# Folding a block-diagonal feature map into two projection weights: pairs of 64-row TensorE tiles with 64 columns in place of four 32-row tiles with 32 columns

## Chip, cores and metric

One core of a Trainium2 chip. The metric is the device time of one execution in microseconds (us). All runs whose times are compared by a ratio are in the fast state, and the granted TensorE clock was 0.998 to 1.0 in them; one execution of the kernel before, at a clock of 0.562 and 354.4 us, is left out. Experiments 9 to 11 are single runs, whose state is unknown: 10 and 11 had a clock of 1.0, and 9 had 0.984, for a reason told there. Single runs of the same kernel lie up to 1.7 us apart.

## The reference, cut to what matters

```python
q, k, v = (qkv[0], qkv[1], qkv[2])            # x @ wqkv, S = 2048, D = 512, 32 heads of 16
pq = jnp.einsum('bhsd,hdf->bhsf', q, w_phi)   # one 16 x 16 feature map per head
pk = jnp.einsum('bhsd,hdf->bhsf', k, w_phi)
phi_q = concatenate([softmax(pq), softmax(-pq)])   # phi_k likewise
...                                            # linear attention, then a gMLP branch and a gate
```

As `(x @ wq) @ w_phi = x @ (wq @ w_phi)`, the kernel folds `w_phi` into the two weights once, and never computes q or k. The "fold" is this small product, done for wk and for wq: 512 x 512 times a block-diagonal matrix with blocks of 16 x 16.

## The kernel before

```python
NT = 16; NDT = 4; P = 128; CH = 512            # 16 row tiles of 128, 4 slices of D
halves = [slice(64 * h, 64 * h + 64) for h in range(2)]
# wqkT: transposed wq and wk; wphi: w_phi as 4 block-diagonal tiles of 128 x 128, zeros elsewhere
...
def fold(qk):
    dst = (wq_p if qk == 0 else wk_p)[:].rearrange("p dt n -> p (dt n)").rearrange(
        "p (m r f) -> p r m f", r=4, f=32)
    pair = zp_tile()                            # two PSUM banks, from the ring of the z tiles
    banks = [pair[:, 0, :], pair[:, 1, :], pq_tile([P, CH])[:, :], pq_tile([P, CH])[:, :]]
    for m in range(NDT * NDT):
        dt, kc = divmod(m, NDT)
        for r in range(4):                      # four row tiles, one bank each
            rows = slice(32 * r, 32 * r + 32)
            nc.tensor.matmul(
                banks[r][:, m * 32:(m + 1) * 32],
                lhsT=wqkT[rows, qk * 4 + kc, dt * P:(dt + 1) * P],
                rhs=wphi[rows, kc, rows], start=True, stop=True)
    ...                                         # ScalarE copies the pair now, the other two banks later
```

The fold for wk lies among the z2 matmuls (L191) at about 26 us, the one for wq at about 36. Later in the kernel, ScalarE stores the output in bursts of four tiles and then goes on with the exponentials of the q projection:

```python
def ba_store(acc, tt, c0=0, c1=D, on_dve=False, on_sp=False):
    ...
        nc.scalar.activation(out=ob[:, :], in_=acc, func=AF.Copy, scale=g_inv[:, tt:tt + 1])   # L531
        (nc.sync if on_sp else nc.scalar).dma_start(out=dst, in_=ob[:, :])                     # L532
...
def ba_step(tt):
    ...
    if tt == group[-1]:                         # groups of four row tiles
        for t in group:
            ba_rem(accs[t][:, :], t)
        attn_tile_64(tt + 2)
        for t in group:
            ba_store(accs[t][:, :], t)          # four stores from ScalarE's own queue
...
for i in range(NT - 1):
    if i + nq < NT:
        q_tile(i + nq, bank_tile(q_bank))       # L355 matmuls, L359 exponentials; one bank for all q tiles
    gg_next(...)                                # L454
    ...
```

## Time and profile before

| view | figure |
|---|---|
| time | 206.62 us, median of 3 runs (206.25 to 206.85) |
| span of the profiled execution | 204.5 us |
| TensorE busy | 98% of the span, 95% of the chain that ended last |
| both folds on that chain | 2 x 0.59 us |
| instructions, all engines | 3978 |
| transfers of instructions on DMA queue q8 | 12, of 16,384 bytes each |

How to read it: TensorE is the bound from end to end, so a change counts by what it does to the moments at which TensorE's matmuls start. The lines themselves are in the prediction. The last row of the table played no part in the prediction, and should have.

### The profile page before, as it was taken

The numbers are of one execution on the slowest core, as the hardware profiler recorded it, in microseconds if no ns is written. First come the engines' busy times: TensorE is split into PE (matmuls) and PEld (weight loads), VectorE is DVE, ScalarE is ACT, GpSimd is POOL, SyncE is SP. The second block draws the span as 40 slices with busy tenths as digits, with TensorE's granted clock in tenths as the row PEclk, the third lists the DMA queues.
The fourth block names the chain that finished last, engine by engine and source line by source line (L and its number), as shares of the span: only waits on it lengthen the run. The fifth ranks groups of instructions, "written<-read, shape, count | busy, mean of one in ns | idle before, by whom it ended". The sixth has DMA issues, their size and how long they took to land.

```text
span 204.5 us, 3978 instructions
## 1 busy us (share of the span) xinstructions
PE 199.6 (98%) x1539; PEld 119.7 (59%) x1557; DVE 130.4 (64%) x283; ACT 74.6 (36%) x122; POOL 45.7 (22%) x76
## 2 busy tenths in 40 slices
PE   7999999999999999999999999999999999999994
PEld 3666666655665555656565666555555555665642
DVE  4467484837977587979797789555566645633332
ACT  3466678796222333332424042222351136002303
POOL 3020202021523325334242442222204220200000
PEclk9999999999999999999999999999999999999999
DMA  6997599999998027940422229763568458652833
GB/s 184 269 209 133 118 237 212 239 216 217 235 276 185 3 38 179 290 93 16 75 48 45 51 38 119 139 124 70 100 161 80 90 113 183 63 96 51 156 64 104
DMA packets 89932, 27.22 MB, mean 133 GB/s; under 512 B 84185, under 2 KB 89913, under 8 KB 89913
## 3 DMA queue, kind: packets, MB, share of 16 engines
q1 hardware_dynamic: 87600, 24.81, 63.1%
q10 hardware_dynamic: 2312, 2.16, 3.7%
q8 instruction: 12, 0.20, 0.4%
q14 instruction: 8, 0.06, 0.1%
HBM read 4.15 MB, written 2.10 MB: 31 GB/s over the span
## 4 chain that ended last, share of the span: by engine, by line
PE 95%; DMA 2%; issue 1%; SPq 0%; DVE 0%
PE mm L454 37%; PE zp L191 18%; PE mm L355 13%; PE mm L515 8%; PE mm L395 7%; PE mm L509 7%; DMA w_z<-in_B_w_in_dram 2%; PE kvacc L411 2%; PE at L467 2%; PE mm L520 1%; PE zp L307 0%; PE at L478 0%; SPq L117 0%; SPq L119 0%; PE pq L307 0%
## 5 line engine op out<-in xcount | busy, mean ns | idle before, releaser
L454 PE MATMUL mm<-z2all,wspT 128*128 128x344 bf16 x512 | 79.9, 309 | 0.0
L454 PEld LDWEIGHTS <-wspT 128*128 128x128 bf16 x512 | 49.0, 98 | 25.3
L191 PE MATMUL zp<-w_z,xT 128*128 128x344 bf16 (+1 forms) x254 | 38.1, 310 | 0.3 <-DMA w_z<-in_B_w_in_dram 0.3
L359 ACT ACTIVATE eq<-mm 128x512 bf16<-128x512 f32 x32 | 17.4, 594 | 51.4 <-PE mm L355 25.7
L363 DVE TENSOR_REDUCE zs<-eq 128x64 f32<-128x1024 bf16 x16 | 19.5, 1220 | 20.0 <-ACT eq L359 20.0
L191 PEld LDWEIGHTS <-xT 128*128 128x128 bf16 x254 | 24.4, 98 | 12.1 <-issue 0.3
L359 ACT ACTIVATE ek<-mm 128x512 bf16<-128x512 f32 x32 | 17.3, 601 | 27.1 <-PE mm L355 27.1
L459 DVE SCALAR_TENSOR_TENSOR ucat<-mm,bT,z1all 128x344 bf16<-128x344 f32 x32 | 17.4, 544 | 15.1 <-PE mm L454 15.1
L372 POOL TENSOR_TENSOR eq<-eq,ratio 128x512 bf16<-128x512 bf16 x16 | 16.9, 1055 | 44.6 <-DVE ratio L371 36.6
L531 ACT ACTIVATE ob<-mm,g_inv 128x512 bf16<-128x512 f32 (+1 forms) x15 | 10.1, 679 | 33.1 <-PE mm L520 28.5
L363 DVE TENSOR_REDUCE zs<-ek 128x64 f32<-128x1024 bf16 x16 | 19.2, 1208 | 2.8 <-ACT ek L359 2.8
L515 PE MATMUL mm<-wspT,uT 128*128 128x512 bf16 (+2 forms) x85 | 20.1, 367 | 0.0
L355 PEld LDWEIGHTS <-xT 128*128 128x128 bf16 x128 | 12.2, 98 | 12.0
L372 POOL TENSOR_TENSOR ek<-ek,ratio 128x512 bf16<-128x512 bf16 x16 | 16.9, 1055 | 2.2 <-DVE ratio L371 1.7
L395 PE MATMUL mm<-wv_sb,xT 128*128 128x512 bf16 x64 | 16.4, 380 | 0.0
L355 PE MATMUL mm<-wq_p,xT 128*128 128x512 bf16 x56 | 16.0, 380 | 0.4
L355 PE MATMUL mm<-wk_p,xT 128*128 128x512 bf16 x61 | 16.1, 379 | 0.2
L509 PE MATMUL mm<-wspT,oT 128*128 128x512 bf16 (+2 forms) x61 | 15.6, 365 | 0.4
L209 DVE BATCH_NORM_STATS2 bn<-z2all 128x6 f32<-128x344 bf16 x32 | 14.9, 502 | 0.0
L206 ACT ACTIVATE z2all<-zp 128x688 bf16<-128x688 f32 x16 | 11.8, 743 | 7.6 <-PE zp L191 7.6
L260 ACT ACTIVATE z1all<-zp 128x688 bf16<-128x688 f32 x16 | 11.9, 743 | 5.1 <-PE zp L191 4.7
L515 PEld LDWEIGHTS <-uT 128*128 128x128 bf16 x85 | 8.1, 98 | 9.4 <-issue 0.2
(77 smaller groups left out, 142.0 us busy)
## 6 DMA issues: line engine op xcount, KB each, us to landing
out_dram<-ob ACTq DMA_DIRECT2D x12, 128.0 KB, 2.4
wspT<-in_B_w_out_dram SPq DMA_DIRECT2D x2, 640.0 KB, 4.9
w_z<-in_B_w_in_dram SPq DMA_DIRECT2D x2, 344.0 KB, 5.0
wv_sb<-in_A_wqkv_dram SPq DMA_DIRECT2D x2, 256.0 KB, 4.4
wspT<-in_A_wo_dram SPq DMA_DIRECT2D x2, 256.0 KB, 3.9
out_dram<-ob SPq DMA_DIRECT2D x3, 128.0 KB, 1.8
w_z<-in_B_w_in_dram ACTq DMA_DIRECT2D x2, 172.0 KB, 3.7
w_z<-in_B_w_in_dram SPq DMA_DIRECT2D x2, 172.0 KB, 3.8
```

The costliest lines, as they stand in the source:

```text
L191: nc.tensor.matmul(zp[:, j, 0:n], lhsT=xT[:, dt, tt * P:(tt + 1) * P], rhs=wt[:, dt, j * HF:j * HF + n], start=(dt == 0), stop=(dt == NDT ...
L209: nc.vector.bn_stats(out=bn6[:, tt, j, :], in_=z2v[:, j, :])
L260: nc.scalar.activation(out=z1all[:, tt, :].rearrange("p (j n) -> p j n", j=2), in_=zp[:, :, 0:HF], func=AF.Gelu_apprx_tanh,)
L355: nc.tensor.matmul(ps[:, :], lhsT=xT[:, dt, tt * P:(tt + 1) * P], rhs=w[:, dt, :], start=(dt == 0), stop=(dt == NDT - 1))
L359: nc.scalar.activation(out=e[:, :, a, :], in_=ps[:, :].rearrange("p (h f) -> p h f", f=DH), func=AF.Exp, scale=1.0 - 2.0 * a)
L363: nc.vector.tensor_reduce(out=z[:].rearrange("p h a -> p (h a)"), in_=e[:].rearrange("p h a f -> p (h a) f"), axis=AX.X, op=ALU.add,)
L372: nc.gpsimd.tensor_tensor(out=e[:, :, 1, :], in0=e[:, :, 1, :], in1=ratio[:, :, None].to_broadcast([P, H, DH]), op=ALU.mult)
L395: nc.tensor.matmul(v_ps[:, :], lhsT=xT[:, dt, tt * P:(tt + 1) * P], rhs=wv_sb[:, dt, :], start=(dt == 0), stop=(dt == NDT - 1))
L454: nc.tensor.matmul(gp[:, 0:HF], lhsT=wspT[:, st, tt * P:(tt + 1) * P], rhs=z2all[:, st, j * HF:(j + 1) * HF], start=(st == 0), stop=(st == ...
L459: nc.vector.scalar_tensor_tensor(out=ucat[tt % NU][:, c0 + j * HF:c0 + (j + 1) * HF], in0=gp[:, 0:HF], scalar=bT[:, tt:tt + 1], in1=z1all[ ...
L509: nc.tensor.matmul(acc, lhsT=oTs[tt][:, g, :], rhs=wo_t[:, g, c0:c1], start=start and g == 0, stop=stop and g == NG - 1)
L515: nc.tensor.matmul(acc, lhsT=uTs[tt][:, i + ft, :], rhs=w_main[i][:, ft, c0:c1], start=start and ft == 0, stop=False)
```

## The change

A row tile is a matmul on 32 or 64 of the 128 rows that the other matmuls use; a round is one matmul on each of the tiles that run side by side; a weight load is the LDWEIGHTS instruction for the `lhsT` operand, of which the trace has one per matmul (1493 of each in the changed kernel).

The intent: half as many matmuls and weight loads for the same result. A 64-row tile takes four heads at a time, two such tiles run side by side (3 to 4 ns apart in the trace after), and each streams 64 columns; of the four 32 x 32 blocks of `wphi` that it multiplies, the two off the diagonal are zeros.

```diff
@@ -297,24 +297,24 @@
 
     def fold(qk):
         dst = (wq_p if qk == 0 else wk_p)[:].rearrange("p dt n -> p (dt n)").rearrange(
-            "p (m r f) -> p r m f", r=4, f=32)
+            "p (m a f) -> p a m f", a=2, f=64)
         pair = zp_tile()
-        banks = [pair[:, 0, :], pair[:, 1, :], pq_tile([P, CH])[:, :], pq_tile([P, CH])[:, :]]
+        odd = [pq_tile([P, CH])[:, :] for _ in range(2)]
         for m in range(NDT * NDT):
             dt, kc = divmod(m, NDT)
-            for r in range(4):
-                rows = slice(32 * r, 32 * r + 32)
+            cols = slice(m % 8 * 64, m % 8 * 64 + 64)
+            for a, rows in enumerate(halves):
                 nc.tensor.matmul(
-                    banks[r][:, m * 32:(m + 1) * 32],
+                    (odd[m // 8] if a else pair[:, m // 8, :])[:, cols],
                     lhsT=wqkT[rows, qk * 4 + kc, dt * P:(dt + 1) * P],
                     rhs=wphi[rows, kc, rows], start=True, stop=True,
                 )
 
-        def take(out, in_):
-            nc.scalar.copy(out=out, in_=in_.rearrange("p (m f) -> p m f", f=32))
-
-        nc.scalar.copy(out=dst[:, 0:2], in_=pair[:, :, :].rearrange("p r (m f) -> p r m f", f=32))
-        return [lambda: take(dst[:, 3], banks[3]), lambda: take(dst[:, 2], banks[2])]
+        def take(h):
+            nc.scalar.copy(out=dst[:, 1, 8 * h:8 * h + 8], in_=odd[h].rearrange("p (m f) -> p m f", f=64))
+
+        nc.scalar.copy(out=dst[:, 0], in_=pair[:, :, :].rearrange("p r (m f) -> p (r m) f", f=64))
+        return [lambda: take(1), lambda: take(0)]
 
     with tc.manual_schedule(engines={mybir.EngineType.PE, mybir.EngineType.Activation}):
         z2_first_two()
```

Passages that no trace of this case bears out are cut from the recorded prediction, and the cuts are marked: the reading of the two paces (25 and 33 ns), the bounds drawn from it, figures from outside this case, and the cost of a stalled z tile. No term of the sum is cut: it came to -20 to +22 ns per fold, 206.62 plus or minus 0.04, put at 206.6 us. Where columns are divided by 2.4, the trace of the kernel before shows that pace: neighbouring matmuls of 344 columns start 145.8 ns apart, those of 512 columns 215.8, so 0.417 ns per column and 2.5 ns besides. The 8.3 ns of the first rival is a quarter of the 33 ns round; that it is a cost of issue was my assumption and not shown. That weight loads hide rests on the 16 of L478: 93 ns each as recorded, they lie within 0.47 us, and their matmuls hold the chain for 0.19. "Drain" is what a gap between two starts holds beyond the first matmul's own columns.

> **What bounds the kernel now.** I read the page first (busy time, slices, the chain that ended last), then the chain in order of time around the two folds, then the timeline of the fold's own matmuls, and at last ScalarE's part in it.
>
> ```profile
> span 204.5 us, 3978 instructions
> ...
> PE 199.6 (98%) x1539; PEld 119.7 (59%) x1557; DVE 130.4 (64%) x283; ACT 74.6 (36%) x122; POOL 45.7 (22%) x76
> ...
> PEclk9999999999999999999999999999999999999999
> ...
> PE 95%; DMA 2%; issue 1%; SPq 0%; DVE 0%
> ```
>
> TensorE is busy 98% of the span at full granted clock in every slice, and 95% of the chain that ended last is TensorE. So only time taken off TensorE's own stream can shorten the run; anything on another engine counts only if TensorE begins to wait for it. The fold's share of that stream is the next question. The chain in order of time, around the second fold (start us, length us, what):
>
> ```profile
> 26.74 9.45 PE zp L191 x64
> 36.19 0.12 PE zp L307 x2
> 36.31 0.01 PE pq L307 x2
> ...
> 36.76 0.02 PE pq L307 x2
> 36.78 7.12 PE zp L191 x48
> ```
>
> L307 is the fold. It runs twice (for wk at 26.15, for wq at 36.19), and each time it holds the chain for 36.78 - 36.19 = 0.59 us. Both together are 1.18 us, 0.6% of the span. This is the whole stake: a fold that cost nothing at all would save 0.6%, which is under the 2% that makes a verdict of faster. The question left is whether the new form is some tenths of a microsecond shorter or longer.
>
> How the present fold is paced shows in the timeline of the first one (start us, us from first start to last end, engine, line, what, how many):
>
> ```profile
> 26.25 0.18 PE L307 MATMUL zp<-wphi,wqkT 32*128 32x32 bf16 x2
> 26.26 0.17 PE L307 MATMUL pq<-wphi,wqkT 32*128 32x32 bf16 x2
> 26.27 0.17 PE L307 MATMUL zp<-wphi,wqkT 32*128 32x32 bf16 x2
> ...
> 26.50 0.19 PE L307 MATMUL zp<-wphi,wqkT 32*128 32x32 bf16 x2
> 26.52 0.19 PE L307 MATMUL pq<-wphi,wqkT 32*128 32x32 bf16 x2
> 26.53 0.19 PE L307 MATMUL zp<-wphi,wqkT 32*128 32x32 bf16 x2
> ```
>
> Two rows (zp and pq) are one round of the four 32-row tiles. Up to about 26.30 a round takes 25 ns (zp rows start at 26.25 and 26.27; the raw starts are 3 to 4 ns apart within a round, then a pause of 15). From 26.30 on a round takes 33 ns (26.50, 26.53; raw starts 8 to 9 ns apart, with no pause). [...] Nine rounds are in the first regime, seven in the second; from the first start (26.085) to the last (26.559) it is 0.474 us.
>
> What a pair of 64-row tiles does, this kernel shows elsewhere, in the attention product on two halves. Its chain:
>
> ```profile
> 145.53 0.54 PE mm L520 x4
> 146.07 0.19 PE at L478 x16
> 146.26 0.97 PE mm L355 x4
> ```
>
> L478 is 16 matmuls of 64 rows and 34 columns, alternately on the two halves: 0.19 / 8 = 24 to 25 ns per pair of halves, with a raw distance of 3 ns inside a pair. L520 is four matmuls of 64 rows and 512 columns in 0.54 us, where four one after the other take 0.86 us. So the two halves run at once, and the weight loads hide.
>
> [...] 16 matmuls of 344 columns take 2.33 us, 145.8 ns each, against 143.3 + 2.5[...]. [...] here loads of 32, 64 and 128 rows by 128 columns last 91, 93 and 98 ns as recorded, so a 64-row load is no dearer than a 32-row one. [...] the last z2 matmul before the first fold starts at 25.843 and the first fold matmul 0.242 us later, of which 0.143 is its own 344 columns, so some 98 ns are drain; after the fold there are 112 ns from the last start to the next, 13 of them its own 32 columns, so again 98.
>
> **The change part by part.**
>
> Removed: 64 matmuls and 64 weight loads per fold, of 32 rows and 32 columns. Added: 32 of each, of 64 rows and 64 columns. The lower or upper 64 rows of wphi are block diagonal with zeros outside, so the result is the same. The rounds are 16 before and 16 after; what changes is that a round is two matmuls of 64 columns and not four of 32.
>
> Cost of a new round. [...] Streaming is 64 / 2.4 = 26.7 ns per tile[...], plus the 2.5 ns that the 344-column matmuls show: 29.2 ns. A second estimate from the nearest width in the trace: 68 columns on 128 rows, eight in 0.26 us, 32 ns each, 28.3 of them streaming; taken as it stands, that is an upper figure for a round. So 15 steps take 438 to 480 ns, plus 3 for the second tile of the last round: 441 to 483 ns, against 474.
>
> Drain on the way in: unchanged, 98 ns (the same change from 128 rows to a smaller row tile). Drain on the way out: 98 plus the last 64 columns, 26.7 ns, instead of 13.3: 13 ns more.
>
> Sum per fold, from the last start before to the first start after: before 242 + 474 + 112 = 828 ns; after 242 + (441 to 483) + 125 = 808 to 850 ns. So -20 to +22 ns per fold, and -0.04 to +0.04 us for both. The number of instructions saved is real (128 of TensorE's 3,096)[...].
>
> ScalarE's copies: one of 1024 elements and two of 512 per fold, before and after.
>
> ```profile
> L314 ACT CAST wk_p<-pq x2: 580/580/581, 31.0 to 33.4; 128x512 bf16<-128x512 f32 x2
> ...
> L316 ACT CAST wk_p<-zp x1: 1007/1007/1007, 26.8 to 26.8; 128x1024 bf16<-128x1024 f32 x1
> ```
>
> (1007 - 580) / 512 = 0.834 ns per element. [...] I expect 1007 and 580 again. They lie beside TensorE's work in any case.
>
> Moved: the banks hold other parts of the result, but the same copy (the pair of banks) is still first, and the two single banks are still taken later, the second of them first, beside the same z1 tiles. The first use of wk is at 43.7, ten microseconds after its last copy; of wq at 70.0. Nothing waits for either.
>
> So the sum is 206.62 plus or minus 0.04, and I put it at 206.6.
>
> **The rivals.**
>
> First, the fold is issue-bound as a whole, and half the instructions halve it: 32 x 8.3 = 0.27 us in place of 0.47, -0.2 us each, -0.4 in all, some 206.2. For it: the 8.3 ns regime is there. Against it: the 34-column pairs of L478 need 25 ns per pair though issue would allow 16.5[...].
>
> Second, the two halves don't overlap with these operands, or weight loads show: 32 x 29 to 32 = 0.93 to 1.02 us, about +0.5 us each, +1.0 in all, 207.6. Against it: L478 and L520, with halves 3 ns apart.
>
> Third, ScalarE or a bank gets late and TensorE waits. ScalarE is busy 16 of the 20 us from 26 to 46, and the page shows no wait of TensorE for it there. As nothing about its copies changes in size or order, I give this little weight[...].
>
> Fourth, the compiler's order on VectorE and GpSimd shifts a little with the shorter fold. TensorE's wait for both is almost nil now, so this could cost or give some 0.2 us at most, an estimate from the small TensorE idle times (0.4 us the largest group).
>
> **Range and chances.** The mechanism gives a shift far below what runs differ by: before, three runs lie between 206.25 and 206.85. The range therefore is that scatter, widened a little for the first, third and fourth rivals: 206.0 to 207.1. A verdict of faster needs -4.1 us, over three times the whole cost of both folds; slower needs +4.1, four times the second rival. Faster 1%, same 98%, slower 1%.
>
> **What would show it.** In the timeline of the changed kernel, rounds of two 64-row matmuls start 29 to 32 ns apart, evenly, with no second regime, and with 3 to 4 ns inside a round. In the chain each fold holds 0.57 to 0.61 us. ScalarE's copies are 1007 and 580 ns. The gap after the last fold matmul is about 125 ns. A round of 17 ns would prove the first rival, 58 or more the second; a wait of TensorE for ScalarE between 26 and 46 us the third; another order of work on VectorE the fourth. The prediction is wrong if the time leaves 206.0 to 207.1 in undisturbed runs.

## The result, and the profile after

The changed kernel took 206.65 us (median of 6 runs, 206.58 to 207.67), the kernel before 206.45 us (median of 6, 205.94 to 206.85). A ratio here and below is the mean time of one kernel's fast runs over that of the other's of the same rounds, so it is not quite the ratio of the medians: 1.002, 95% interval 0.9996 to 1.0044. By the measure of 2% this is the same, and inside the predicted range. Still the medians moved up by 0.2 us and the means by 0.4, where the working had said 0.04 at most. An unchanged time lies within the interval, so the times alone don't call for a cause. Part of the means' rise is one run, 207.67 us with a span of only 205.0: 1 us more than in the other five lies outside its recorded span, and without it the means differ by 0.24. But the trace did show something.

The page of the changed kernel (its head, busy times, the instruction queue, and the chain by engine):

```profile
span 204.9 us, 3869 instructions
...
PE 200.7 (98%) x1493; PEld 119.9 (58%) x1493; DVE 130.4 (64%) x283; ACT 74.6 (36%) x122; POOL 45.7 (22%) x76
...
q8 instruction: 11, 0.18, 0.4%
...
PE 93%; DMA 2%; ACT 2%; ACTq 1%; SPq 0%; issue 0%; DVE 0%
```

TensorE is still busy 98%. The chain of before had no ScalarE in it; now 2% is ScalarE and 1% its queue. And there is one transfer of instructions fewer. First the folds themselves, in the chain in order of time:

```profile
26.75 9.45 PE zp L191 x64
36.20 0.13 PE zp L307
...
36.77 7.11 PE zp L191 x48
```

and in the timeline of the first fold:

```profile
26.32 0.19 PE L307 MATMUL zp<-wphi,wqkT 64*128 64x64 bf16 x1
26.32 0.19 PE L307 MATMUL pq<-wphi,wqkT 64*128 64x64 bf16 x1
26.35 0.19 PE L307 MATMUL zp<-wphi,wqkT 64*128 64x64 bf16 x1
26.35 0.19 PE L307 MATMUL pq<-wphi,wqkT 64*128 64x64 bf16 x1
```

A round of two matmuls takes 29 ns, evenly through the fold (raw starts 26.318, 26.347, 26.376; 3 to 4 ns within a round). The fold holds the chain for 36.77 - 36.20 = 0.57 us instead of 0.59. From the last z2 matmul's start before a fold to the next one's start after it:

| | into the fold | first to last start | out of the fold | sum |
|---|---|---|---|---|
| before, two folds | 242, 242 ns | 474, 475 | 112, 112 | 828, 829 |
| after, two folds | 243, 242 ns | 450, 451 | 122, 123 | 815, 816 |

So each fold became 13 ns shorter. (The step after that, between the first two z2 matmuls behind a fold, takes 156 to 157 ns instead of the usual 146, in both kernels alike.) ScalarE's copies are what they were, as the lines' own instructions show:

```profile
L314 ACT CAST wk_p<-pq x2: 580/580/580, 31.0 to 33.4; 128x512 bf16<-128x512 f32 x2
...
L316 ACT CAST wk_p<-zp x1: 1007/1007/1007, 26.8 to 26.8; 128x1024 bf16<-128x1024 f32 x1
```

Then where is the rise? I laid TensorE's start times of the two traces side by side, matmul by matmul. The changed kernel starts its steady stream 20 ns late (its first weights landed later), gains 13 + 13 ns at the folds and is 7 ns ahead from 37 us on. At 152 us it falls 0.383 us behind in a single step, and it ends 0.365 us behind. The chain of the changed kernel at that step (start, length, what):

```profile
149.21 0.70 ACT ob L531
...
149.93 0.78 ACTq L532
...
150.84 1.09 ACT eq L359 x2
...
151.98 1.02 PE mm L355 x4
```

and the timelines of ScalarE and of TensorE in the kernel before at the same place:

```profile
149.22 0.69 ACT L531 ACTIVATE ob<-mm,g_inv 128x512 bf16<-128x512 f32 x1 [0.42 <-ACT ob L531]
149.94 0.34 ACTq L532 DMA_DIRECT2D out_dram<-ob  x1
150.40 1.08 ACT L359 ACTIVATE eq<-mm 128x512 bf16<-128x512 f32 x2 [0.49 <-ACT ob L531]
...
151.60 1.03 PE L355 MATMUL mm<-wq_p,xT 128*128 128x512 bf16 x4
```

Up to 149.9 us both are alike to 10 ns. Then the issue of the fourth output store holds ScalarE's queue for 0.78 us instead of 0.34. The two exponentials behind it start at 150.84 instead of 150.40 and end at 151.93 instead of 151.48. They free the one bank of the q projection; before, that was 0.12 us early enough for the next q matmuls (151.60), and now those wait.

Nothing of this touches the fold, 110 us earlier. What differs at that moment is on the DMA queues, between 149 and 151 us. Before:

```profile
q10 hardware_dynamic: 329, 0.30, 46.9%
q1 hardware_dynamic: 550, 0.13, 31.8%
...
out_dram<-ob ACTq DMA_DIRECT2D x2, 128.0 KB, 1.9
```

After:

```profile
q1 hardware_dynamic: 533, 0.13, 82.4%
q10 hardware_dynamic: 135, 0.12, 52.4%
q8 instruction: 1, 0.02, 3.0%
...
out_dram<-ob ACTq DMA_DIRECT2D x2, 128.0 KB, 2.8
```

A transfer of 16,384 bytes of instructions lies among the stores (it starts at 149.36 us and takes 0.97), and the stores land 0.9 us later. The packets of q1, SyncE's transposes at that time, are slower too: as many bytes take 82.4% of the engines' time instead of 31.8%. In the trace of before such transfers lie at 140.16 and 157.10 us, and none meets this burst. (One meets a later burst, at 190.9 us, without cost to TensorE: see after the experiments.)

### The profile page after: what moved, and what is told of

It reads as the page before. It is cut to its first block, busy times and chain, and to the rows that moved or that the text cites. A ratio compares the mean times of both kernels' runs of the same rounds, so it can differ in the third digit from the quotient of the medians.

```text
span 204.9 us, 3869 instructions
## 1 busy us (share of the span) xinstructions
PE 200.7 (98%) x1493; PEld 119.9 (58%) x1493; DVE 130.4 (64%) x283; ACT 74.6 (36%) x122; POOL 45.7 (22%) x76
## 4 chain that ended last, share of the span: by engine, by line
PE 93%; DMA 2%; ACT 2%; ACTq 1%; SPq 0%; issue 0%; DVE 0%
PE mm L454 35%; PE zp L191 18%; PE mm L355 13%; PE mm L515 8%; PE mm L395 7%; PE mm L509 6%; DMA w_z<-in_B_w_in_dram 2%; PE kvacc L411 2%; PE at L467 2%; ACT ob L531 1%; PE mm L520 1%; ACTq L532 1%; ACT eq L359 1%; PE zp L307 1%; SPq L117 0%
## 5 line engine op out<-in xcount | busy, mean ns | idle before, releaser
L515 PE MATMUL mm<-wspT,uT 128*128 128x512 bf16 (+2 forms) x85 | 20.1, 367 | 0.0
L509 PE MATMUL mm<-wspT,oT 128*128 128x512 bf16 (+2 forms) x68 | 16.6, 366 | 0.0
L515 PEld LDWEIGHTS <-uT 128*128 128x128 bf16 x85 | 8.1, 98 | 9.4 <-issue 0.2
```

The lines of the kernel that those rows point to most:

```text
L509: nc.tensor.matmul(acc, lhsT=oTs[tt][:, g, :], rhs=wo_t[:, g, c0:c1], start=start and g == 0, stop=stop and g == NG - 1)
L515: nc.tensor.matmul(acc, lhsT=uTs[tt][:, i + ft, :], rhs=w_main[i][:, ft, c0:c1], start=start and ft == 0, stop=False)
```

## The experiments

Theory A: the changed kernel issues 128 TensorE instructions fewer, so the moments at which TensorE's next block of instructions is fetched move, and one such transfer now meets the store burst; the stall follows from that meeting, not from the fold. Theory B: the long store issue is chance and comes with any kernel. A third view: the new fold causes it in some other way. The kernels of the first four experiments ran on one chip, those of experiments 5 to 8 on a second, 9 to 11 on a third and 12 on a fourth. "Lag" below is TensorE's delay against the first trace of the kernel before, and "stall" the step of the lag at 152 us. "The burst" is the first of three bursts of four stores, from 146.6 to 150.3 us in the kernel before, and the fourth store is its last.

### 1. The kernel before, again

No edit.

> The unchanged kernel before, run again. Theory A (instruction transfers): the trace of the changed kernel has a stall of TensorE of 0.38 us near 151 us, because 128 fewer TensorE instructions move the 16 KB instruction transfers, and one of them (149.36 us) meets the burst of output stores. Then the kernel before never shows it: its instruction transfers are again near 140 and 157 us, its store issues on ScalarE's queue take 0.34 us each, span 204.4 to 204.6. Theory B (chance): the long issue of 0.78 us comes and goes from run to run; then it may show here, and spans scatter over 204.4 to 205.0.

Measured: 206.43 us (6 runs), ratio 1.0003 (0.9988 to 1.0018) to the other runs of the same kernel. Transfers at 140.4 and 157.6 us, the burst's four store issues 0.34 to 0.35 us, no stall. (A store of the last burst, at 191.9 us, took 0.47 to issue, which I had not expected: see below.) Its span of 204.7 is just outside what I had expected: the first weights landed 0.25 us later and the lag stayed at 0.215 to 0.25 to the end. So the start of the kernel scatters by some tenths, and the spans with it.

### 2. The changed kernel, again

No edit.

> The unchanged new kernel, run again. Theory A: every run has the stall: the last of the first four output stores takes about 0.78 us to issue again, an instruction transfer lies at about 149.4 us, TensorE waits about 0.2 us as recorded and loses 0.38 us, span 204.9 to 205.2, ratio to before 1.001 to 1.002. Theory B: some runs at 204.5, ratio within 0.9995 and 1.0005. The folds themselves: 29 ns per pair again in both theories.

Measured: 206.94 us, ratio 1.0025 (1.0005 to 1.0045). The transfer lies at 149.41 us, the fourth store issue took 0.49 us, the stall was 0.093 us. The folds took 815 and 816 ns again. So the stall comes back, but its size varies, which theory A in the form I wrote (0.78 us and 0.38 us each time) did not have; the table after the experiments shows on what the size depends. Its start was 0.39 us late, as in experiment 1 by chance, so its span of 205.0 alone would have misled.

### 3. The old fold, with the instruction stream moved by half a block

```diff
-        warm_up(6)          # 6 matmuls of 512 columns
-        warm_up(1, P)       # 1 of 128
+        warm_up(71, 45)     # 71 of 45: 64 matmuls and 64 weight loads more, 3195 columns for 3200
```

> The old fold of four 32-row tiles, with 128 TensorE instructions more at the very start (the warm-up of 6 x 512 + 128 columns cut into 71 pieces of 45 columns, 3195 columns in place of 3200, while TensorE waits for its first data anyway). [...] Theory A: a transfer lands near 149 us and the stall of about 0.38 us appears although the fold is untouched: span 204.9 to 205.0, ratio 1.001 to 1.003. Theory B or a theory that the new fold itself causes it: span 204.5, ratio 1.000.

Measured: 207.19 us, ratio 1.0037 (1.0018 to 1.0057). The transfer came at 149.68 us, and ScalarE's timeline (lines are one lower here) shows the long issue under the old fold:

```profile
149.59 0.69 ACT L530 ACTIVATE ob<-mm,g_inv 128x512 bf16<-128x512 f32 x1 [0.41 <-ACT ob L530]
150.31 0.77 ACTq L531 DMA_DIRECT2D out_dram<-ob  x1
151.21 1.09 ACT L358 ACTIVATE eq<-mm 128x512 bf16<-128x512 f32 x2 [0.93 <-ACT ob L530]
```

The lag steps from 0.363 to 0.742 us at 152 us: a stall of 0.379 us, within 4 ns of the changed kernel's. The other 0.34 us of lag had come at 10.5 us, at a wait for weights, with an extra transfer of instructions at 8.56 us. So the stall is about half of the lag of this profiled execution, and the ratio is not the stall's alone. This run is what sets theory A apart: the fold is untouched and the stall is there. (By half a block is meant: in the kernel before, from 89.0 to 190.9 us, about 255 recorded TensorE instructions start from one transfer to the next, 221 to 285 in six intervals, and 128 are half of that. The reason recorded for it is cut, as no trace shows it.)

### 4. The new fold, with the same move

The edit of experiment 3 on the changed kernel, which brings the count of TensorE instructions ahead of the burst back to that of the kernel before.

> The new fold with the same 128 extra instructions at the start, so the count of TensorE instructions before the store burst is that of the kernel before. Theory A: transfers back near 140 and 157 us, no long store issue, no stall, span 204.45 to 204.55, ratio 0.9990 to 1.0005. If the new fold itself caused the stall, it stays: 204.9.

Measured: 206.54 us, ratio 1.0006 (0.9990 to 1.0022). Transfers at 139.6 and 157.6 us, and

```profile
150.39 0.34 ACTq L531 DMA_DIRECT2D out_dram<-ob  x1
150.85 1.08 ACT L358 ACTIVATE eq<-mm 128x512 bf16<-128x512 f32 x2 [0.49 <-ACT ob L530]
...
192.15 0.86 ACTq L531 DMA_DIRECT2D out_dram<-ob  x1
```

no long issue in the burst and no stall (the last line, of the last burst, is taken up after the experiments); the lag is 0.450 us from 46 us to the end, all of it from a late start (0.478, less 0.028 for the folds). The span of 205.0 that I had not expected is that start. The folds took 815 ns each.

### 5. The new fold, moved by a quarter of a block

```diff
+        warm_up(39, 82)     # in place of the two lines; 64 instructions more
```

> The new fold with 64 more TensorE instructions at the start (warm-up in 39 pieces of 82 columns), a quarter of an instruction transfer. The transfer that lay at 149.4 us should come about 4.4 us earlier (a quarter of the 17.4 us between two), at about 145.0, before the four output stores at 146.6 to 150.3. Theory A (a transfer inside the store burst makes the stall): store issues 0.34 to 0.35 us, no stall, ratio 0.9995 to 1.0015. If any position but that of the kernel before is bad: a stall of 0.3 to 0.4 us.

Measured: 206.58 us, ratio 0.9997 (0.9978 to 1.0016). The transfer lay at 144.3 us (expected 145.0), ahead of the burst; store issues 0.34 to 0.37 us; no stall.

### 6. The new fold, moved by three quarters

```diff
+        warm_up(103, 31)    # 192 instructions more
```

> The new fold with 192 more TensorE instructions at the start (103 pieces of 31 columns). The transfer should come about 13 us earlier than 149.4, at 136.3, and the next at about 153.5, after the burst. Theory A: no long store issue, no stall near 151 us; ratio 0.9995 to 1.0015.

Measured: 207.65 us, ratio 1.0055 (1.0033 to 1.0077), a miss. The part at the burst came as said: transfers at 138.2 and 154.3 us, store issues 0.34 to 0.36, no stall. But this kernel lost 1.0 us at the start, between 6.71 and 7.74 us (a wait for z2's weights), and 0.2 at 8.56 (a wait for x); a transfer of instructions lies at 5.7 us, amid the first loads, where the kernel before has its first at 15.7. All four runs, in the fast state by their clocks, took long (207.46 to 208.19), so the loss is no chance. That the transfer at 5.7 us makes it is the likely reading, not one that I isolated: the warm-up differs too.

### 7. The changed kernel, with the last store of a group on SyncE's queue

```diff
-                ba_store(accs[t][:, :], t)
+                ba_store(accs[t][:, :], t, on_sp=t == group[-1])
```

> The new kernel, with only the last of each group's four output stores issued from SyncE's queue instead of ScalarE's. The instruction transfer stays at about 149.4 us. If the stall reaches TensorE through ScalarE's queue (the long issue holds up the two exponentials that free the bank of the q projection), it goes: TensorE goes on at about 151.6 in step with the rest, ratio 0.9990 to 1.0010, although the transfer still meets the burst. If the transfers to TensorE or the transposes are slowed themselves, some stall of 0.1 to 0.4 us stays. A rival cost: SyncE's queue is busy with transposes from 147.8 to 152.5, so the store comes late, without harm to TensorE as its buffer is needed some 20 us later.

Measured: the transfer at 149.8 us, the store issue now on SyncE (0.37 us), no stall; the lag is -0.019 us at 46 us and -0.022 at the end, so inside its span this profiled execution beat the kernel before by what the folds gave. Its time was the longest of the four all the same, as 3.3 us of it lie outside the span of 204.5 (experiment 12 comes back to this). The times were 206.19 to 207.84 us in four runs, ratio 1.0016 (0.9983 to 1.0049): inconclusive, and therefore run again as experiment 12.

### 8. The old fold moved by half a block, with the last store on SyncE's queue

The edits of experiments 3 and 7 on the kernel before.

> The old fold with the 128 extra instructions, which stalled by 0.38 us near 152 us in its run, now with the last store of each group on SyncE's queue. Theory A with the way through ScalarE's queue: the transfer stays near 149.5 us, the stall of 0.38 us goes; ratio 1.000 to 1.003 (the extra transfer at 8.6 us may still cost about 0.3 us at the start). Otherwise the stall stays and the ratio is 1.003 to 1.005.

Measured: 206.81 us, ratio 1.0007 (0.9992 to 1.0022). The transfer lay at 149.6 us, no stall (lag 0.218 us from 46 us on, 0.222 at the end). The wait at 10.5 us that cost experiment 3 0.34 us did not come here either, so the lower ratio is not the stall's alone.

### 9 and 10. Each fold three times over

```diff
-        for m in range(NDT * NDT):
+        for m in [m for m in range(NDT * NDT)] * 3:
```

> The old fold done three times over (same result). If the second pace of 33 ns per round of four is that of issue[...], all later rounds keep it: 48 rounds, first to last start 474 + 32 x 33 = 1,530 ns. If the 33 ns were a passing effect, rounds return to 25 ns: about 1,280 ns.

> The new fold done three times over. Every round of two stays at 29 ns[...]: 48 rounds, first to last start 450 + 32 x 29.1 = 1,381 ns. [...]

Measured, one execution each: old fold 219.21 us, new fold 208.35, kernel before on the same chip 206.31. The rounds of the old fold run: 39, then seven of 25 ns, a passage of 32 and 38, and then 32 to 34 ns for all of the next 36 rounds: the second pace stays. What sets it is not shown. But the last round of the first fold came 4.94 us after the one before, and the second fold lost 2.62 us in one round in the same way, which no theory of mine had. After each gap the z matmuls ran at half pace for a while (287 ns apart instead of 146, at a granted clock of 0.50 from 32 to 35 us), and the mean clock was 0.984. The weight loads' timeline, old fold:

```profile
26.03 1.59 PEld L307 LDWEIGHTS <-wqkT 32*128 32x128 bf16 x187 [0.28 <-issue]
32.45 0.13 PEld L307 LDWEIGHTS <-wqkT 32*128 32x128 bf16 x5 [4.83 <-issue]
```

and new fold:

```profile
26.24 1.46 PEld L307 LDWEIGHTS <-wqkT 64*128 64x128 bf16 x96 [0.28 <-issue]
```

TensorE went through 374 instructions in 1.6 us and then, as I read it, had none: the next transfer of instructions was recorded from 29.86 to 31.04 us, after TensorE stopped at 27.6, amid transposes on q1 that kept the DMA engines busy (nine tenths or more in every 0.2 us from 27.8 to 30.6), and TensorE went on 1.4 us after its end. The second gap (45.3 to 47.9 us) has a transfer from 45.26 to 46.59. The new fold three times over has 192 instructions in place of 384 and no gap: from first to last start 1,384 ns (expected 1,381), all rounds but the first 29 to 30 ns. So 29 ns is the lasting pace of these rounds, as the matmuls of 344 and 512 columns would have it (64 x 0.417 + 2.5 = 29.2). The store burst, 2 us later here, met a transfer at 151.0 us: the fourth issue took 0.46 us, and TensorE lost 0.06.

### 11. The fold without row tiles

```diff
+        for dt in range(NDT):
+            for kc in range(NDT):
+                nc.tensor.matmul(
+                    (pair[:, dt, :] if dt < 2 else odd[dt - 2])[:, kc * P:(kc + 1) * P],
+                    lhsT=wqkT[:, qk * 4 + kc, dt * P:(dt + 1) * P],
+                    rhs=wphi[:, kc, :], start=True, stop=True)
```

> The fold without row tiles: 16 matmuls of 128 rows and 128 columns. [...] no drains of 98 ns, but 16 x (53.3 + 2.5) = 893 ns of streaming: from the last start before to the first start after 146 + 893 = 1,039 ns, against 828 of the old fold and 815 of the new. Both folds together cost 0.4 us more than either.

Measured: 1,040 ns for each fold, 207.07 us in one execution (206.31 before). A late start gives 0.41 us of its lag of 0.81, and the folds 2 x 0.20: 212 ns each up to the first start behind a fold, less the 11 ns of the slow step behind row tiles, which does not come here (146 ns). Row tiles are worth 0.2 us per fold, even with the drains.

### 12. Experiment 7 once more

> The new fold with each group's last store on SyncE's queue, once more with more rounds, as its four runs scattered from 206.19 to 207.84. Profile again without a stall near 151 us while an instruction transfer lies at about 149.5. If the long store issue was the only loss of the changed kernel, the ratio to before is 0.999 to 1.001; if a late store on SyncE's queue or another meeting at the start costs as much, it stays at 1.001 to 1.003.

Measured: 207.09 us (6 runs, 206.73 to 207.73), ratio 1.0041 (1.0019 to 1.0063). In the profile the meeting is there again (transfer at 149.4 us), and the store's issue on SyncE's queue is again a long one:

```profile
150.31 0.57 SPq L532 DMA_DIRECT2D out_dram<-ob  x1
```

but TensorE doesn't notice: in its timeline

```profile
150.90 1.24 PE L515 MATMUL mm<-wspT,uT 128*128 128x512 bf16 x5
151.98 1.03 PE L355 MATMUL mm<-wq_p,xT 128*128 128x512 bf16 x4
```

the q matmuls follow the L515 group without a wait, and the lag is 0.377 us before and after. So the way of the stall is shown: a slow issue, of 0.57 us, cost nothing here, where ScalarE's queue didn't hold it. The times are not better for it, though. Part lies outside the recorded span: time less span is 1.7 to 2.7 us here, mean 2.15, against 1.67 to 1.78 in the fast runs of the kernel before in the same call. In the profiled executions of experiments 3, 7 and 12 a last transfer of instructions lies at 205.8, 206.8 and 205.4 us, after the end; but time less span was 3.3 us only in 7, and 1.7 in 3 and 12. What costs there stays open. This version is not a gain.

Of the first burst:

| kernel | transfer near the burst | fourth store's issue | end of that issue, after the transfer's end | stall |
|---|---|---|---|---|
| before; again | 140.2, 157.1; 140.4, 157.6 us | 0.34; 0.34 us | | 0; 0 us |
| changed; again | 149.4; 149.4 | 0.78; 0.49 | 0.39; 0.32 us | 0.383; 0.093 |
| old fold moved by half (3) | 149.7 | 0.77 | 0.38 | 0.379 |
| new fold moved by half (4) | 139.6, 157.6 | 0.34 | | 0 |
| new fold, a quarter (5), three quarters (6) | 144.3; 138.2, 154.3 | 0.34; 0.34 | | 0; 0 |
| changed, store on SyncE (7, 12) | 149.8; 149.4 | 0.37; 0.57, on SyncE | before it; 0.38 | 0; 0 |
| old fold moved, store on SyncE (8) | 149.6 | 0.37, on SyncE | before it | 0 |
| new fold three times (10) | 151.0 | 0.46 | 0.26 | 0.06 |

The two later bursts limit what may be concluded. A transfer meets the last one in six profiles, both of the kernel before among them (190.9 and 191.0 us): one store's issue takes 0.47 to 0.86 us there, the longest in experiment 4, and TensorE's lag does not move. It meets the middle one in experiments 6 and 11 (172.9 and 172.4 us), some 0.6 us ahead of the fourth issue as in the changed kernel, and that issue takes 0.34. So a meeting doesn't always lengthen an issue, and a long issue doesn't always cost TensorE time. But all eleven long issues of all traces end 0.26 to 0.39 us after a transfer's end, so in these traces how long one gets goes with when the transfer ends.

## Why the prediction was right, and what it missed

**The bound and the stake.** Right: the time did not move by 2%, and 206.65 us is within 206.0 to 207.1. That it lies so near to the 206.6 is in part luck: with more runs the kernel before came to 206.45, not the 206.62 on which the forecast stood, and a loss that I had not foreseen made up for it. All 1.18 us of both folds would not have been enough for a verdict.

**The round.** Right: 29.1 ns, the lower of the two estimates (29.2), with 3 to 4 ns within a round and no second pace. The estimate of 32 ns from the 68-column matmuls was too high, so it should not have been carried as an equal bound. A first step of 38 to 39 ns, which both folds have, I had not put into the new one.

**Drains.** Right: 242 to 243 ns into the fold, 122 to 123 out of it (125 predicted); at 0.417 ns per column that is some 99 and 96 ns beyond the last matmul's own columns. Experiment 11, without row tiles, has no such gap: 1,040 ns where 1,039 were expected without one. The 11 ns of the next step, which experiment 11 without row tiles does not have, were not counted, but are the same before and after.

**The sum of the fold.** Right: 815 to 816 ns, in the predicted 808 to 850, and 26 ns saved in both folds.

**The second pace of the old fold.** The pace is right, and shown to last by experiment 9: about 33 ns for 36 rounds on end. That issue sets it, on which the first rival rested, was my assumption; no run shows it.

**ScalarE's copies, the order on the other engines.** Right: 1007 and 580 ns, with runs of 64 elements as with runs of 32; the order of work on VectorE, GpSimd and SyncE is the same.

**What it missed.** The sentence "So the sum is 206.62 plus or minus 0.04" left out a term. I counted the removed instructions only by their time on TensorE, and not as bytes that have to be fetched while other transfers run. Removing 128 of them put a fetch into the first store burst, which cost 0.09 to 0.38 us in the two profiles, more than the 0.026 us that the folds gave. None of my four rivals was this; the third came nearest (TensorE waiting for ScalarE), but placed it between 26 and 46 us. The range held because I had set it by the scatter of runs. The clue was there to be read: the kernel before's page lists a queue of kind "instruction", with 12 transfers, and by the trace each is of 16,384 bytes and about 255 TensorE instructions from the next. Experiments 2 and 4 show the rest: 128 instructions more moved the transfer from 149.4 us to 139.6, about half of the 17 to 18 us between two.

**What stays open.** Why the store's issue waits for the instruction transfer is not shown, only that the two go together: with a transfer in the first burst, the issue was 0.12 to 0.44 us longer in all four profiles with it on ScalarE's queue, and 0.2 us longer in one of three with it on SyncE's; without one, no store's issue was long in any burst. Nor is it shown why a meeting in the middle burst lengthened no issue. Whether the whole of the 0.2% in the ratios of the changed kernel (1.0020 and 1.0025) is this stall can't be told from intervals of half a per cent; that moving the stream takes the ratio to 1.0006 and 0.9997 speaks for it.

## What to carry to other kernels

Before trading many small matmuls for fewer larger ones, take the paces from the trace: that of the old round as it runs (here 25 ns for nine rounds and 33 from then on), and for the new one an estimate from the columns (here 64 x 0.417 + 2.5 = 29.2 ns, with both figures from the matmuls of 344 and 512 columns; 29.1 measured). The gain is the old round's pace less the new one's, here 33 and 25 ns against 29, and not the ratio of instruction counts. And when a change alters the number of instructions, look at where the instruction transfers fall afterwards: a difference of a few tenths of a microsecond far from the change may be a fetch that met another transfer, and padding the stream without touching the change tells the two apart. And look for gaps after bursts of very short matmuls: in experiment 9, 374 TensorE instructions in 1.6 us were followed by 4.8 us without any, with a transfer of instructions in that gap.
